# First group of two chunks, first batch's k and q ahead of v, another engine sequence in the MLP, two chunks a step in short tiles

## The chip, the core and the metric

The kernel runs on one core of a Trainium2 chip. The metric is the time of one execution on the device, in microseconds (us); the median over runs is compared. The engines are TensorE (PE in the profile, with its weight loads as PEld), VectorE (DVE), ScalarE (ACT), GpSimd (POOL) and SyncE (SP, which here issues nearly all DMAs). Each engine takes its own instructions in the order in which they are written.

## What is computed

Inputs are q, k, v of shape (4, 8, 576, 64), and weights. Heads 0 to 3 attend to the 32 latest positions, heads 4 to 7 to every fourth of the 128 latest. Two MLPs follow, over 2304 tokens.

```python
attn = softmax(where(mask, q @ k.T / 8, -1e9)) @ v     # batch 4, heads 8, 576 x 64
x = attn.transpose(0, 2, 1, 3).reshape(2304, 512)
h = x @ w_in                                           # 512 -> 2048
x = (h - tanh(h)) @ w_out                              # 2048 -> 512
out = (((x @ w1) * (x @ w2)) @ w3) @ wo                # 512 -> 1024 -> 1024 -> 512
```

## The kernel before

All matrix products of the MLPs are made of three: each operand stands as an upper part (`hi`, rounded to fp32r) and a lower part (`lo`, the rest), and hi·hi, hi·lo and lo·hi are added in PSUM (`mm3`).

**Weights** arrive as 64-bit floats, 512 KB a tile, and are converted on the core. One conversion is: a DMA into one of two `stage` buffers (`load64`), an absolute value on ScalarE (`cv_abs`, L105), four bit operations of 512 columns on VectorE (`cv_bits`, L110, L114, L120, L123), the upper part on ScalarE (L128) and the lower part on GpSimd (L129). `tick` moves this chain on by one stage: it splits the tile whose bits are done, does the bits of the next one, issues a load, and takes the absolute value of a loaded tile. There are 72 tiles. Their parts need two slots each; 16 slots (`WG`) exist from the start, 18 more (`LT`) come when attention's buffers are closed, and slots come free again when a tile has been used for the last time.

**Attention** is cut into 24 units, six for each batch (two kinds of heads, three blocks of positions). One unit has a k tile and a q tile (`load_q`, two DMAs, 224 KB at most and 384 KB), a v tile (`load_v`, two or four DMAs, 384 KB), scores on TensorE (`at_scores`: 1 mask product and 24 pairs of small matmuls), maximum and subtraction on VectorE (`at_max`), exp on ScalarE, the sum and its reciprocal on VectorE and the scaling on GpSimd (`at_norm`), three transposes on TensorE (`at_T`), their copy on ScalarE, the product with v on TensorE (`at_pv`), and its two parts written to X by ScalarE and VectorE (`at_evac`). An `attn_slot` does one stage each for four units that follow each other. k, q and v have three buffers each, so a load for unit n+3 waits until unit n has used its own.

**The first MLP** goes over 16 chunks of 128 hidden columns in four groups, `GS = (3, 4, 4, 5)`. For each group it goes over tiles of tokens, and in each tile over the group's chunks. The first group has six tiles of 256 tokens and two of 384, and its steps alternate with attention slots (`due` counts them); the other groups have four tiles of 512 and one short tile of 256. One step i is: 12 matmuls into `h` (`st_h`, L415), tanh on ScalarE (L449), h minus tanh on VectorE (`st_g`, L455), its upper part on ScalarE (L457), its lower part on VectorE (`st_glo`, L464; on GpSimd while attention runs), and, behind the next step's `st_h`, 12 matmuls into `y` (`st_y`, L492). After a tile's last chunk `y` is copied to Y (first group, L503 and L505) or added to it on VectorE (L507).

`start_up` handles the first batch's attention, and then this loop takes over:

```python
st_h(i)
st_tanh(i)
st_g(i)
st_glo(i)
...
if i:
    st_y(i - 1)
...
if g or i < 3 or i >= 18 or i % TE == 0:
    tick()
```

**The second MLP** first multiplies w3 and wo (8 steps of 24 matmuls), and then goes over five tiles of tokens with 8 steps each: two products into `h` (L415), their product on VectorE (L678), its parts (L680, L681) and 12 matmuls into the output (L697). The conversions that are left run beside its first tile.

## Time and profile before

| | us |
|---|---|
| median of 3 runs | 859.16 (858.43 to 860.78) |
| the profiled execution | 861.07 |
| its span | 859.3 |
| TensorE busy in the span | 819.1 |
| VectorE busy | 483.9 |
| ScalarE busy | 293.8 |
| GpSimd busy | 133.0 |

The span runs from the first to the last instruction; 1.77 us of the profiled execution lie around it. Busy time of TensorE includes stretches in which a matmul took longer than it must, so what TensorE loses is read from the times at which products start.

### The profile page before, as it was taken

The page shows a single profiled execution, that of the slowest core. Times are in us where ns is not written, and L with a number is a line of the kernel's source. Part 1 is how long each engine was busy: PE and PEld are TensorE (multiplying, and loading weights), DVE is VectorE, ACT ScalarE, POOL GpSimd, SP SyncE. Part 2 cuts the span into 40 slices and gives each one's busy share as a digit, 9 for nine tenths or more (in the row PEclk, how much of TensorE's full clock was granted, in tenths as well). Part 3 has the DMA queues.
Part 4 walks back from the last instruction along what each step waited for, and adds up shares of the span by engine and source line. Part 5 has one row for each costly group of instructions (what it writes and reads, how often), then busy time and mean ns, then how long its engine had stood idle before and what let it go on. Part 6 is the DMA issues. An engine that isn't in the chain of part 4 may idle for free.

```text
span 859.3 us, 13590 instructions
## 1 busy us (share of the span) xinstructions
PE 819.1 (95%) x5568; PEld 688.7 (80%) x5574; DVE 483.9 (56%) x789; ACT 293.8 (34%) x557; POOL 133.0 (15%) x120
## 2 busy tenths in 40 slices
PE   7588999999999999999999979999999999999998
PEld 4477999877789788888888878886788888888897
DVE  5588654888735873378888885577612212222121
ACT  3545655444422432234343333333311211211121
POOL 2243232222100210012211131222100000000000
PEclk9789999999999999999999999999999999999999
DMA  9978851222300320012322322133010010010010
GB/s 258 270 216 237 231 169 39 74 99 98 99 1 6 107 84 1 1 50 99 98 74 74 99 98 73 50 99 109 14 50 1 0 50 1 1 49 1 1 50 25
DMA packets 36511, 67.74 MB, mean 79 GB/s; under 512 B 4320, under 2 KB 24928, under 8 KB 36448
## 3 DMA queue, kind: packets, MB, share of 16 engines
q1 hardware_dynamic: 35456, 66.60, 25.5%
q8 instruction: 44, 0.72, 0.3%
q10 hardware_dynamic: 992, 0.26, 0.1%
q14 instruction: 19, 0.16, 0.1%
HBM read 62.13 MB, written 4.72 MB: 78 GB/s over the span
## 4 chain that ended last, share of the span: by engine, by line
PE 65%; DVE 21%; DMA 6%; ACT 5%; issue 2%; SPq 0%; ACTq 0%; DVEq 0%
PE h L415 37%; PE y L492 14%; PE o L697 10%; DVE a L110 4%; DVE a L114 3%; DVE a L120 3%; DVE a L123 3%; DVE th L455 2%; DVE gs L464 2%; ACT gs L457 2%; DMA st<-in_w 2%; PE x L353 2%; DMA v<-in_vt 2%; PE s L293 1%; DVE Y L507 1%
## 5 line engine op out<-in xcount | busy, mean ns | idle before, releaser
L415 PE MATMUL h<-X,LT 128*128 128x512 f32 (+1 forms) x576 | 131.3, 368 | 0.0
L492 PE MATMUL y<-gs,WG 128*128 128x256 f32 (+2 forms) x648 | 123.3, 338 | 5.0 <-DVE Y L507 3.0
L415 PE MATMUL h<-WG,X 128*128 128x512 f32 (+1 forms) x441 | 120.3, 375 | 0.0
L492 PEld LDWEIGHTS y<-gs,WG 128*128 128x128 f32 x648 | 102.4, 189 | 20.2 <-ACT WG L128 2.2
L415 PEld LDWEIGHTS h<-X,LT 128*128 128x128 f32 x576 | 101.5, 188 | 18.0
L415 PE MATMUL h<-X,WG 128*128 128x256 f32 (+2 forms) x567 | 113.9, 341 | 2.1 <-ACT X L369 1.2
L678 DVE TENSOR_TENSOR a_sb<-h,a_sb 128x512 f32<-128x512 f32 (+1 forms) x40 | 25.5, 638 | 158.5 <-PE h L415 152.3
L415 PEld LDWEIGHTS h<-X,WG 128*128 128x128 f32 x567 | 91.8, 196 | 11.7 <-ACT X L369 1.5
L492 PE MATMUL y<-gs,LT 128*128 128x512 f32 (+1 forms) x420 | 93.9, 373 | 5.7 <-ACT gs L457 4.6
L415 PEld LDWEIGHTS h<-WG,X 128*128 128x128 f32 x441 | 83.2, 189 | 15.2
L492 PEld LDWEIGHTS y<-gs,LT 128*128 128x128 f32 x420 | 74.4, 192 | 20.4 <-ACT gs L457 5.6
L455 DVE TENSOR_TENSOR th<-h,th 128x512 f32<-128x512 f32 (+2 forms) x89 | 52.1, 585 | 66.4 <-ACT th L449 66.3
L105 ACT ACTIVATE a<-st 128x512 f32<-128x512 f32 x72 | 48.5, 673 | 100.4 <-DMA st<-in_w 48.6
L457 ACT ACTIVATE gs<-th 128x512 fp32r<-128x512 f32 (+2 forms) x89 | 49.0, 550 | 92.9 <-DVE th L455 92.9
L449 ACT ACTIVATE th<-h 128x512 f32<-128x512 f32 (+2 forms) x89 | 45.4, 510 | 76.3 <-PE h L415 75.9
L464 DVE TENSOR_TENSOR gs<-th,gs 128x512 fp32r<-128x512 f32 (+2 forms) x71 | 44.9, 632 | 46.2 <-ACT gs L457 45.2
L415 PE MATMUL h<-LT,X 128*128 128x512 f32 (+1 forms) x198 | 60.6, 375 | 0.0
L114 DVE TENSOR_SCALAR a<-a 128x512 uint32<-128x512 uint32 x72 | 58.0, 805 | 2.5
L110 DVE TENSOR_SCALAR a<-a 128x512 f32<-128x512 f32 x72 | 59.0, 819 | 0.5 <-ACT a L105 0.5
L129 POOL TENSOR_TENSOR X<-a,X 128x512 fp32r<-128x512 f32 x26 | 35.6, 1367 | 130.5 <-ACT X L128 119.0
L123 DVE SCALAR_TENSOR_TENSOR a<-st,a 128x512 uint32<-128x512 uint32 x72 | 54.2, 753 | 2.5
L120 DVE SCALAR_TENSOR_TENSOR a<-st,a 128x512 uint32<-128x512 uint32 x72 | 53.6, 744 | 2.4
(69 smaller groups left out, 990.3 us busy)
## 6 DMA issues: line engine op xcount, KB each, us to landing
st<-in_w SPq DMA_DIRECT2D x32, 512.0 KB, 3.4
q<-in_qz SPq DMA_DIRECT2D x24, 384.0 KB, 5.1
st<-in_w_in SPq DMA_DIRECT2D x16, 512.0 KB, 3.5
st<-in_w_out SPq DMA_DIRECT2D x16, 512.0 KB, 3.5
v<-in_vt SPq DMA_DIRECT2D x32, 192.0 KB, 5.3
st<-in_wo SPq DMA_DIRECT2D x8, 512.0 KB, 3.4
k<-in_kT SPq DMA_DIRECT2D x16, 224.0 KB, 5.2
v<-in_vt SPq DMA_DIRECT2D x16, 128.0 KB, 3.6
```

What stands on the lines that cost most here:

```text
L105: nc.scalar.activation(out=a.bitcast(F32), in_=st[:, :, 1].bitcast(F32), func=ACTF.Abs)
L110: nc.vector.tensor_scalar(out=a.bitcast(F32), in0=a.bitcast(F32), scalar1=2.0 ** -15, scalar2=CMAX, op0=ALU.max, op1=ALU.min,)
L114: nc.vector.tensor_scalar(out=a, in0=a, scalar1=3, scalar2=0x3FFFFFFF, op0=ALU.logical_shift_left, op1=ALU.bitwise_and,)
L120: nc.vector.scalar_tensor_tensor(out=a, in0=st[:, :, 1], scalar=0xC0000000, in1=a, op0=ALU.bitwise_and, op1=ALU.bitwise_or)
L123: nc.vector.scalar_tensor_tensor(out=a, in0=st[:, :, 0], scalar=29, in1=a, op0=ALU.logical_shift_right, op1=ALU.bitwise_or)
L415: nc.tensor.matmul(out=ps, lhsT=a[sel[0]], rhs=b[sel[1]], start=(i == 0), stop=(i == n - 1), **kw)
L449: nc.scalar.activation(out=th[:, :tn], in_=gst[i][:, :tn], func=ACTF.Tanh)
L455: nc.vector.tensor_tensor(out=th[:, :tn], in0=ps[:, :tn], in1=th[:, :tn], op=ALU.subtract)
L457: nc.scalar.activation(out=gs[:, 0, :tn], in_=th[:, :tn], func=ACTF.Copy)
L464: eng.tensor_tensor(out=gs[:, 1, :tn], in0=th[:, :tn], in1=gs[:, 0, :tn].bitcast(F32), op=ALU.subtract)
L492: nc.tensor.matmul(out=y[k], lhsT=wt[sel[0]][:, 128 * k:128 * k + 128], rhs=gs[:, sel[1], :tn], start=(c == 0 and n == 0 and (not packed o ...
L697: nc.tensor.matmul(out=ps, lhsT=cs[:, e, 128 * m:128 * m + 128], rhs=WW[j][f], start=(j == 0 and n == 0), stop=(j == NJ - 1 and n == 2),)
```

## The change

- The first group has two chunks, the third five: `GS = (2, 4, 5, 5)`. The number of steps in the first group falls from 24 to 16, and 1.5 times as many attention slots stand in each.
- At the start, k and q of the first five units are issued ahead of any v; no buffer has to come free for them, since `homes` puts the first batch's v tiles, and k and q of its units 3 to 5, into parts of Y that nothing else uses yet. The first batch's attention is written out as a string of words (s scores, M maximum, E exp, N norm, T transposes, C copy, P product, O evacuation, a and b the two halves of the bit operations, f the split, z a spinning matmul). Unit 5 of the first batch moves into the slots behind.
- Mask tables and a copy of the identity are cast on GpSimd (before on VectorE and ScalarE), and ScalarE issues 10 DMAs for them (before 6).
- `tick` takes the slots before the bit operations, and unless `later` is set it splits the tile in the same call. In the second to fourth group it is called between `st_g` and `st_glo`. In a slot the transposes come ahead of the product with v.
- In short tiles of the second to fourth group a step takes two chunks: two times 12 matmuls into two halves of one `h` tile, then one tanh, one subtraction and one lower part of 512 columns, then two times 12 matmuls into `y`.
- In the second MLP's first tile the two calls of `tick` stand behind each other.

```diff
-GS = (3, 4, 4, 5)
+GS = (2, 4, 5, 5)
...
-    def tick():
+    def split():
+        key, a, hi, lo = bitsed.popleft()
+        cv_hi(a, hi)
+        cv_lo(a, hi, lo)
+        W[key] = (hi, lo)
+    def tick(later=False):
         if bitsed:
-            key, a = bitsed[0]
-            if len(free) - (reserve[0] if key[0] in ("w1", "w2") else 0) >= 2:
-                bitsed.popleft()
-                hi, lo = free.popleft(), free.popleft()
-                cv_split(a, hi, lo)
-                W[key] = (hi, lo)
-        if absed and not bitsed:
+            split()
+        if absed and len(free) - (reserve[0] if absed[0][0][0] in ("w1", "w2") else 0) >= 2:
             key, st, a = absed.popleft()
             cv_bits(st, a)
-            bitsed.append((key, a))
+            bitsed.append((key, a, free.popleft(), free.popleft()))
         prefetch()
         if loaded and not absed:
             key, st = loaded.popleft()
             absed.append((key, st, cv_abs(st)))
+        if bitsed and not later:
+            split()
...
-        attn_pools["pp"] = st.enter_context(tc.tile_pool(name="pp", bufs=3))
+        attn_pools["pp"] = st.enter_context(tc.tile_pool(name="pp", bufs=4))
...
-        for j in range(4):
-            r = slice(HQ * j, HQ * j + HQ)
-            nc.scalar.dma_start(out=m[r, 1:], in_=masks[r, 1:, 32 * (j % 2):32 * (j % 2) + HW])
+        nc.scalar.dma_start(out=id_sb, in_=ident)
         nc.scalar.dma_start(out=m[:, 0], in_=masks[:, 0, :HW])
-        nc.scalar.dma_start(out=id_sb, in_=ident)
+        for a in (slice(1, 2), slice(2, 6)):
+            for j in range(4):
+                r = slice(HQ * j, HQ * j + HQ)
+                nc.scalar.dma_start(out=m[r, a], in_=masks[r, a, 32 * (j % 2):32 * (j % 2) + HW])
...
+            nc.gpsimd.tensor_copy(out=mask_sb[:, to], in_=src)
+
+        if part == 0:
+            nc.gpsimd.tensor_copy(out=id16_sb, in_=id_sb)
+            put(slice(9, 10), m[:, 0:1])
+            put(slice(10, 13), m[:, 1:2])
+            return
...
+        if of_v:
+            if n < PB:
+                k, a = (0, wq * n) if n < 3 else (n - 2, c0)
+                return Y[:, k, a:a + wq].rearrange("p (h t c) -> p h t c", h=2, t=TU)
+            return attn_pools["kv"].tile([128, 2, TU, 2 * D], F32, tag="v", name="v")
+        if 3 <= n < PB:
+            a = Y[:, n - 2, c0 - wk - wq:c0]
+            k = a[:, :wk].rearrange("p (e k) -> p e k", e=2)
+            q = a[:, wk:].rearrange("p (e t c) -> p e t c", e=2, t=TU)
+        else:
...
+        if on[2]:
+            at_T(n - LAGT)
...
         if on[2]:
-            at_T(n - LAGT)
+            at_Tcopy(n - LAGT)
         if on[3]:
             at_evac(n - LAGP)
         if on[0]:
             at_max(n)
-        if on[2]:
-            at_Tcopy(n - LAGT)
-        if on[0]:
             at_exp(n)
...
+            w = 2 if g and tn == 256 else 1
+            for c in range(0, GS[g], w):
+                cs = list(range(c, min(c + w, GS[g])))
+                steps.append((g, ti, t0, tn, cs, ti == len(tiles) - 1))
...
+        for m, c in enumerate(cs):
+            key = ("in", sum(GS[:g]) + c)
+            wi = [w.rearrange("p (k f) -> p k f", k=KC) for w in W[key]]
+            mm3(ps[:, tn * m:tn * m + tn], [
+                ([w[:, k, :] for w in wi], [X[:, 2 * k + e, t0:t0 + tn] for e in range(2)])
+                for k in range(KC)
+            ], start=m == 0, skip_group_check=len(cs) > 1)
...
+        order = [(m, n, k) for m in range(len(cs)) for n in range(3) for k in range(KC)]
+        if cs[0] == 0 or cs[-1] == GS[g] - 1:
+            order.sort(key=lambda mnk: mnk[2])
...
-        ld(0)
-        load_q(0)
-        load_q(1)
-        load_q(2)
-        load_v(0)
-        ld(1)
-        prep_masks()
-        for part in range(2):
-            bits(0, part)
-        fin(0)
...
-        for n in range(PB + LAGP - 1):
-            if n < PB:
-                at_scores(n)
-                load_q(n + 3)
...
-            if n == 1:
-                load_v(2)
-                ld(2)
...
+        run("q0 w0 q1 q2 q3 q4 v0 v1")
+        run("m0 a0 b0 f0 m1")
+        run("w2 v2 v3 v4 w1 q5 v5")
+        run("""
+            s0 z1 s1 M0 E0 z1 M1 E1 s2 z1 N0 s3 M2 E2 z1 N1 T0 C0 z1 s4 M3 E3 T1 C1 P0 O0
+            N2 M4 E4 T2 C2 P1 N3 T3 C3 P2 a2 N4 O1 T4 C4 P3 b2 O2 P4 f2 a1 O3 O4 b1
+        """)
+        run("q6 q7 v6 v7")
...
-        slot[0] = PB
-        first[:] = [PB, PB, PB, PB - 1]
+            if m == 1:
+                hi, lo = free.popleft(), free.popleft()
+                bitsed.append((key, ab[m], hi, lo))
+        slot[0] = PB - 1
+        first[:] = [PB - 1] * 4
...
+                if g:
+                    tick()
+                elif i == 0:
+                    tick(True)
+                elif i == 1 and bitsed:
+                    split()
                 st_glo(i)
-                if i < 2:
-                    tick()
-                due += 0.75 if i < 6 else 0.5
+                due += 1.125 if i < 4 else 0.75
...
-            due += 0.75 if i < 6 else 0.5
+            due += 1.125 if i < 4 else 0.75
...
-            if g or i < 3 or i >= 18 or i % TE == 0:
-                tick()
+            if g == 0 and (i >= 12 or i % 2 == 0):
+                tick(True)
...
             nc.scalar.activation(out=hi, in_=ps, func=ACTF.Copy)
+            tick()
             nc.vector.tensor_tensor(out=lo, in0=ps, in1=hi.bitcast(F32), op=ALU.subtract)
...
-            tick()
...
                     tick()
+                    tick()
...
-            tick()
```

SyncE, in the start, from the second weight tile on: what it issues in the kernel before (`st` is a weight tile, `k`, `q`, `v` are attention's).

```order
L100 DMA st<-in_w_out 128x1024
L249 DMA k<-in_kT 128x2x192
L253 DMA q<-in_qz 128x2x384
L272 DMA v<-in_vt 64x2x384 x2
L249 DMA k<-in_kT 128x2x224
L253 DMA q<-in_qz 128x2x384
L272 DMA v<-in_vt 64x2x384 x2
L100 DMA st<-in_w_in 128x1024
L249 DMA k<-in_kT 128x2x224
L253 DMA q<-in_qz 128x2x384
```

And in the changed kernel, from the third unit's k and q on (`Y` stands for the parts of Y that hold k, q and v for a time).

```order
L274 DMA k<-in_kT 128x2x224
L277 DMA q<-in_qz 128x2x384
L274 DMA Y<-in_kT 128x2x192
L277 DMA Y<-in_qz 128x2x384
L274 DMA Y<-in_kT 128x2x224
L277 DMA Y<-in_qz 128x2x384
L296 DMA Y<-in_vt 64x2x128
L296 DMA Y<-in_vt 64x2x256
L296 DMA Y<-in_vt 64x2x128
L296 DMA Y<-in_vt 64x2x256
L296 DMA Y<-in_vt 64x2x384 x2
L100 DMA st<-in_w_in 128x1024
```

Before, v of unit 1 stands behind k and q of unit 3, and a second weight tile ahead of both; now five units' k and q, then two units' v, then the second weight tile.

VectorE, from one step to the next of the second group in the kernel before: the four bit operations stand behind the lower part `gs` of a step.

```order
L464 TENSOR_TENSOR gs<-th,gs 128x512
L110 TENSOR_SCALAR a<-a 128x512
L114 TENSOR_SCALAR a<-a 128x512
L120 SCALAR_TENSOR_TENSOR a<-st,a 128x512
L123 SCALAR_TENSOR_TENSOR a<-st,a 128x512
L455 TENSOR_TENSOR th<-h,th 128x512
```

And one step in the changed kernel:

```order
L490 TENSOR_TENSOR th<-h,th 128x512
L110 TENSOR_SCALAR a<-a 128x512
L114 TENSOR_SCALAR a<-a 128x512
L120 SCALAR_TENSOR_TENSOR a<-st,a 128x512
L123 SCALAR_TENSOR_TENSOR a<-st,a 128x512
L499 TENSOR_TENSOR gs<-th,gs 128x512
```

The four bit operations moved between the subtraction `th` and the lower part `gs` of the same step.

VectorE, in the short tile of the fourth group in the kernel before: a conversion stands between any two pairs of 256 columns.

```order
L455 TENSOR_TENSOR th<-h,th 128x256
L464 TENSOR_TENSOR gs<-th,gs 128x256
L110 TENSOR_SCALAR a<-a 128x512
L114 TENSOR_SCALAR a<-a 128x512
L120 SCALAR_TENSOR_TENSOR a<-st,a 128x512
L123 SCALAR_TENSOR_TENSOR a<-st,a 128x512
L455 TENSOR_TENSOR th<-h,th 128x256
L464 TENSOR_TENSOR gs<-th,gs 128x256
```

And in the changed kernel, the short tile's second and third step:

```order
L490 TENSOR_TENSOR th<-h,th 128x512
L110 TENSOR_SCALAR a<-a 128x512
L114 TENSOR_SCALAR a<-a 128x512
L120 SCALAR_TENSOR_TENSOR a<-st,a 128x512
L123 SCALAR_TENSOR_TENSOR a<-st,a 128x512
L499 TENSOR_TENSOR gs<-th,gs 128x512
L490 TENSOR_TENSOR th<-h,th 128x256
L110 TENSOR_SCALAR a<-a 128x512
L114 TENSOR_SCALAR a<-a 128x512
L120 SCALAR_TENSOR_TENSOR a<-st,a 128x512
L123 SCALAR_TENSOR_TENSOR a<-st,a 128x512
L499 TENSOR_TENSOR gs<-th,gs 128x256
```

A conversion now stands in a step of two chunks, whose two operations are 512 columns wide, and one in the last step of one chunk; the short tile has three steps in place of five, and two conversions in place of four.

## Rows read from the trace of the kernel before

**Rows 1.** Stretches: length, busy us of PE, PEld, DVE, ACT, POOL; clock, DMA, GB/s
```profile
0.00:42.00 42.00, 26.00 (x460) 17.10 (x467) 22.53 (x51) 17.43 (x36) 10.74 (x15) 0.86 0.95 265
42.00:86.00 44.00, 37.52 (x709) 32.96 (x708) 37.58 (x76) 23.16 (x52) 17.36 (x18) 0.90 0.80 227
86.00:147.00 61.00, 61.00 (x1104) 56.00 (x1102) 34.10 (x85) 34.95 (x79) 17.56 (x23) 1.00 0.55 154
147.00:172.00 25.00, 23.41 (x138) 22.09 (x132) 19.39 (x30) 11.04 (x23) 5.82 (x5) 1.00 0.20 64
172.00:230.00 58.00, 56.23 (x247) 45.59 (x248) 49.87 (x71) 25.11 (x46) 14.52 (x11) 1.00 0.30 100
```

**Rows 2.** Timeline of the start: start, length, engine, line, operation, idle before and its releaser
```profile
28.45 0.88 PE L293 MATMUL s<-k,q 128*32 128x64 f32 x48 [2.73 <-DMA q<-in_qz]
31.37 1.50 SPq L272 DMA_DIRECT2D v<-in_vt  x2
37.55 1.55 PE L353 MATMUL x<-pb,v 128*64 128x64 f32 x24 [2.24 <-DVE X L370]
41.56 2.50 PE L415 MATMUL h<-X,WG 128*128 128x256 f32 x10 [1.21 <-ACT X L369]
```

**Rows 3.** Timeline of TensorE: the first 384-column product
```profile
147.06 2.35 PE L415 MATMUL h<-X,WG 128*128 128x384 f32 x12
```

**Rows 4.** Chain of work that ended last: start, length, engine, tile, line
```profile
92.86 1.44 PE h L415 x12
98.14 1.44 PE h L415 x12
231.41 2.72 PE h L415 x12
```

**Rows 5.** Timeline of the short tile that ends the fourth group
```profile
486.39 1.59 PE L415 MATMUL h<-X,WG 128*128 128x256 f32 x12
503.55 1.70 PE L492 MATMUL y<-gs,LT 128*128 128x256 f32 x12 [1.53 <-ACT gs L457]
508.01 2.96 PE L492 MATMUL y<-gs,LT 128*128 128x256 f32 x12 [2.76 <-ACT gs L457]
510.77 1.03 PE L415 MATMUL h<-LT,X 128*128 128x512 f32 x2
```

**Rows 6.** Timeline of VectorE and GpSimd in the second group
```profile
199.53 1.29 POOL L129 TENSOR_TENSOR WG<-a,WG 128x512 fp32r<-128x512 f32 x1 [4.07 <-PE h L415]
199.57 1.53 DVE L110 TENSOR_SCALAR a<-a 128x512 f32<-128x512 f32 x1
207.32 0.42 DVE L110 TENSOR_SCALAR a<-a 128x512 f32<-128x512 f32 x1
```

**Rows 7.** Groups of instructions by form: count, busy us, mean ns, idle before
```profile
L110 DVE TENSOR_SCALAR a<-a 128x512 f32<-128x512 f32 x72 | 59.0, 819 | 0.5 <-ACT a L105 0.5
L120 DVE SCALAR_TENSOR_TENSOR a<-st,a 128x512 uint32<-128x512 uint32 x72 | 53.6, 744 | 2.4
L464 DVE TENSOR_TENSOR gs<-th,gs 128x512 fp32r<-128x512 f32 x52 | 36.0, 692 | 36.3 <-ACT gs L457 36.3
L305 DVE TENSOR_TENSOR pm<-s,ms 128x384 f32<-128x384 f32 x24 | 13.4, 558 | 2.2
L317 DVE RECIPROCAL ms<-ms 128x6 f32<-128x6 f32 x24 | 4.6, 191 | 0.8
L464 POOL TENSOR_TENSOR gs<-th,gs 128x256 fp32r<-128x256 f32 x18 | 13.2, 735 | 49.6 <-ACT gs L457 37.8 <-issue 11.8
L105 ACT ACTIVATE a<-st 128x512 f32<-128x512 f32 x72 | 48.5, 673 | 100.4 <-DMA st<-in_w 48.6 <-DMA st<-in_w_in 21.3 <-DMA st<-in_w_out 17.9
```

**Rows 8.** Timeline of TensorE at the start of the third group
```profile
284.87 3.00 PE L492 MATMUL y<-gs,LT 128*128 128x512 f32 x12 [1.08 <-DVE Y L507]
```

**Rows 9.** Waits of the whole run: us in total, times, longest
```profile
PE y L492 <- DVE Y L507: 4.1, 5, 1.3
```

**Rows 10.** Chain of work that ended last, in the second MLP's first tile
```profile
575.84 3.34 DMA st<-in_w
```

More of the change, by code (lines that the diff above doesn't have):

```diff
@@ L415, in mm3 @@
                 nc.tensor.matmul(
[L416 removed]
+                    out=ps, lhsT=a[sel[0]], rhs=b[sel[1]], start=(start and i == 0), stop=(i == n - 1), **kw
                 )
@@ L476, in st_y @@
     def st_y(i):
-        g, ti, t0, tn, c, last = steps[i]
-        need(("out", sum(GS[:g]) + c))
-        wt = W["out", sum(GS[:g]) + c]
+        g, ti, t0, tn, cs, last = steps[i]
+        need(*[("out", sum(GS[:g]) + c) for c in cs])
         packed = g == 0 and ti < 6
-        if c == 0:
+        if cs[0] == 0:
             gst["y"] = y_ps(tn)
```

129 lines of the change are left out of this document (54 added, 75 removed).

## The prediction

> **What bounds the kernel now.** I read the busy time by stretches first, then the timeline of each stretch in which TensorE is short of work, then the chain that ended last. From 230 us on TensorE stands nearly gapless: 12 matmuls of 512 columns take 2.72 us there, and in the first group's steady part a step with one attention slot takes 98.14 - 92.86 = 5.28 us, of which its two products take 1.44 each, so a slot costs TensorE 2.40 [rows 4]. A step of 512 columns is then 5.44 us and one of 256 is 2.88; for 384 I take the middle, 4.16. Whatever is over these figures is loss, and four places hold nearly all of it.
>
> The start, up to the first 384-column product at 147.06 [rows 3]. Until then there are 24 slots and 35 products of 256 columns (18 `h`, 17 `y`): 24 x 2.40 + 35 x 1.44 = 108.0. So 39.1 are lost. To 42 us the DMA engines are busy 95% of the time at 265 GB/s, the granted clock averages 0.86 (so it lay at the lower of its two levels, 1.2 of 2.4 GHz, for a part), and TensorE works 26 of 42 us; from 42 to 86 VectorE is busy 37.6 of 44 us, and after 86 no loss is left [rows 1]. In the start the scores wait 2.73 for a q, unit 4's v is issued only at 31.37, behind q tiles of the second batch, its product starts at 37.55 and the first `h` runs from 41.56 [rows 2].
>
> From 147 to 230 VectorE is the engine that is late: 69.3 of 83 us busy. The 138 matmuls of the first 25 us (12 of 256 columns, 126 of 384) need 23.3, the 247 of the next 58 (18 of 384, 229 of 512) need 55.0 [rows 1, 4], so 4.7 are lost.
>
> The short tile that ends the fourth group. From 486.39 to 510.77 stand five `h` and five `y` of 256 columns and one `y` of 512: 10 x 1.44 + 2.72 = 17.1 of 24.4 us; 7.3 are lost, with TensorE waiting up to 2.76 for the lower part's step [rows 5]. VectorE has a whole conversion there in each 2.88 us.
>
> At tile ends `y` waits for the additions to Y, 4.1 us in five places [rows 9]; one is 1.08 at the third group's start [rows 8].
>
> **The change, part by part.** The sum is made against the profiled execution, 861.07, which lies 1.9 above the median of the runs; I take 1.9 off at the end.
>
> *TensorE's own work.* The first group loses six steps of 256 and two of 384, the others gain four tiles of 512 and one of 256: -6 x 2.88 - 2 x 4.16 + 4 x 5.44 + 2.88 = -1.0. Two chunks in a step change no matmul.
>
> *Start-up.* Five units (about 1.02 MB each from the shapes) and three weight tiles of 0.52 MB must land before the first `h`: 6.65 MB, 25.1 us at 265 GB/s [rows 1], from 1.2 us on, and I add 1.7 for the last landing: 28. Behind that last tile (word w1 of the string) ScalarE takes its absolute value (0.67) ahead of units 3 and 4's evacuation, and VectorE two bit operations and two lower parts (0.42 each, 0.55 each) [rows 6, 7]. So the first `h` at about 30.5, where it now starts at 41.56. If that tile or ScalarE's ten DMA issues come later it is 34; if data flow at the rate of full DMA share, 28. The mask casts on GpSimd have no row. Each has 64 to 192 columns, so one costs between nothing and the 0.74 of a 256-column pass of two inputs [rows 7]; three of them stand ahead of the first scores, 0 to 2.2. I take 0: VectorE converts the first weight tile ahead of the first maximum anyway, and that is the cover; without it the 2.2 would fall on the path. The Trainium skill ("GPSIMD Engine Reference", Performance versus the Vector engine) speaks against this move: it has GpSimd about half as fast as VectorE on an elementwise pass. No run here shows that ratio for a cast; by it the three would cost an estimated 1.5, and the sum would be 1.5 higher were they on the path.
>
> *First group.* What remains from the first `h` to the first 384-column product is 24 x 2.40 + 23 x 1.44 = 90.7, less five slots already done: 78.7 for TensorE alone. VectorE has in that stretch 19 units with four passes of about 0.55 (the row with 0.558 stands for four alike) and two small ones of 0.19: 2.58 each, 49.0; 12 subtractions and 10 copies of 256 columns at about 0.4 (estimated from 0.69 for 512), 8.8; and five conversions of 3.12 each (two bit operations near 0.82, two near 0.75), 15.6: 73.4 in all [rows 7]. Between 42 and 86, the stretch now that is packed most like it, VectorE reached 85% [rows 1], so I take 73.4 / 0.854 = 86. The first 384-column product then starts at 30.5 + 86 = 116.5. TensorE alone would allow 109; at 75% for VectorE it is 128. The DMAs of 24 units and 8 weight tiles, 28.6 MB, need 108 us at 265 GB/s, so they follow close behind and do not set it.
>
> A conversion costs 3.12, and not the 2.2 of two passes at 0.42 and two at 0.69, because GpSimd's lower part runs into it: beside it L110 took 1.53, alone 0.42 [rows 6]. The Trainium skill ("SBUF — State Buffer", Who interferes with whom) makes this a lock: a VectorE pass in a mode that uses both of its ports, or with two SBUF inputs, and a GpSimd pass that reads SBUF keep each other out for a whole instruction. The two rows agree with that. In the first group `tick(True)` still splits ahead of the bits, so by rule and rows the price stays there; if the overlaps fell away the stretch would be 5 shorter.
>
> *147 to 230.* Two chunks of the second group instead of one are converted before it starts, and a conversion in a step no longer meets GpSimd's lower part, which now follows it. A step with a conversion then holds VectorE for 2.2 + 2 x 0.69, plus 0.7, its share of four additions in four steps: 4.3 against 5.44 [rows 6, 7]. I take 4 off of the 4.7 (between 2 and 4.7).
>
> *Short tiles.* One conversion now stands beside 5.76 us of TensorE's work, and VectorE needs 3.6 for it. I take 6.3 off of the 7.3; the last step has one chunk and still a conversion. Of the waits for Y, 2.4 (1.08 and 1.28 at two group starts).
>
> *Lower part behind the conversion.* From the end of `h` the third part of `y` needs tanh (0.67 at most, by the absolute value of as many columns), subtraction 0.69, bits 2.2, lower part 0.69 and some 0.3 of gaps, 4.6 [rows 6, 7]; TensorE has two other products, 5.44, in between. What is queued behind the bits on VectorE, the additions to Y, ends some 0.4 before the next tile's `y` asks. I charge 1.0 for all tile ends.
>
> *Second MLP.* A cycle of the first tile hangs on a load that waits for a stage buffer, 3.34 to land [rows 10]; two `tick`s in a row leave it, and one more conversion falls into it: I charge 1.5 (0 to 3).
>
> Sum: 116.5 + (861.07 - 147.06) + (4 x 5.44 + 2.88 - 2 x 4.16 = 16.3) - 4 - 6.3 - 2.4 + 1.0 + 1.5 = 836.6, against the median 1.9 less: 834.7, so 835.
>
> **The rivals.**
>
> *TensorE sets the first group.* The transposes ahead of the product with v and four `pm` buffers let VectorE run at over 93%; the product at 109, the whole 7.5 less: 827. For it speaks the gapless stretch from 86 on [rows 1]; against it that no conversions ran there. Chance 0.22.
>
> *The first group stays as slow as VectorE or the loads make it.* More slots in a step put more GpSimd passes against the conversions, and SyncE's queue holds q and v behind a weight load that waits for VectorE. Then the product comes at 125 to 129 and the time is 843 to 848. For it speaks 42 to 86 [rows 1]. Chance 0.22.
>
> *The tiles' ends keep their stalls*, as the last step of one chunk and the group starts are still late: start as forecast, 6 of 8.7 given back, 841. Chance 0.07; with it go small mishaps of the start.
>
> *Slower: the lower part comes too late for `y` in the second to fourth group.* The place is L499 behind the four bit operations. It decides from a chain of 5.9 us on (5.44 and the 0.45 until the third matmul at tile ends), that is if a conversion takes 3.6 in place of 2.2, as when GpSimd blocks two of its four passes. To undo all of the gain of 24 it would have to wait 0.6 in each of some 39 steps with a conversion, a chain of 6.5; with 0.7 the time is 862. Against it: the lower part of the tile before ends long before the next bits. Chance 0.04.
>
> **How the numbers follow.** The forecast has 0.45: 835, its own range 830 to 841. The range of 8 in 10 goes from 823 (first 384-column product at 107 to 109, all losses gone, no charge) to 850 (that product at 128, half the charges more). A measurement of this kernel tells some 0.3%, 2.6 us. All cases but the last are faster by far more; for the last and for what I have not seen I give slower 0.04 and the same 0.03.
>
> **What would show it.** Right: first `h` near 30 and the first 384-column product near 116; no TensorE wait over 1 us in the fourth group's short tile; L110 near 0.42 in the second to fourth group and up to 1.5 in the first. Wrong: the first product over 34, VectorE under 80% in a first group that is still late, or `y` waiting for L499 in steady steps.

## The result and the profile after

The changed kernel takes 866.65 us (median of 8 runs, 862.25 to 868.12), the kernel before, run beside it, 859.81. The ratio is 1.0073, 95% interval 1.0054 to 1.0092: slower by 0.7%, where the forecast was 835 and faster, with a range of 823 to 850. The profiled execution took 865.26, 28.7 over the sum of 836.6 that was made for it.

The first product and the first 384-column product in the changed kernel's timeline (start, duration, engine, line; in brackets the idle time before and what ended it):

```profile
35.73 1.24 PE L442 MATMUL h<-X,WG 128*128 128x256 f32 x3
...
140.04 2.35 PE L442 MATMUL h<-X,WG 128*128 128x384 f32 x12 [1.18 <-DVE X L399]
```

They answer to 41.56 and 147.06 before [rows 2, 3]; at 41.56 start ten of the first product's 12 matmuls, the other two ran at 39.58, so the start was 3.9 earlier by its first matmul. The changed kernel by stretches (busy time of each engine, granted clock, DMA share, GB/s), which answers to [rows 1]:

```profile
0.00:36.00 36.00, 24.36 (x406) 15.81 (x411) 17.17 (x39) 13.80 (x26) 10.36 (x21) 0.88 0.92 263
36.00:140.00 104.00, 86.88 (x1720) 74.33 (x1720) 71.38 (x161) 53.80 (x123) 32.33 (x37) 0.94 0.72 197
158.00:180.00 22.00, 18.02 (x67) 14.07 (x66) 15.44 (x26) 9.53 (x17) 5.40 (x4) 0.84 0.31 95
180.00:230.00 50.00, 50.00 (x222) 41.40 (x221) 30.61 (x52) 19.11 (x31) 9.03 (x7) 1.00 0.25 74
490.00:515.00 25.00, 23.93 (x162) 22.12 (x161) 19.73 (x37) 9.91 (x17) 6.46 (x5) 1.00 0.33 106
580.00:620.00 40.00, 36.03 (x147) 27.80 (x146) 27.20 (x39) 15.67 (x27) 10.26 (x8) 0.96 0.25 79
```

TensorE's longest waits over the whole span (waiting tile and line, what ended the wait: us in total, times, longest):

```profile
PE t L355 <- POOL pm L342: 14.6, 8, 2.4
PE t L355 <- DMA Y<-in_vt: 6.4, 2, 3.2
PE o L714 <- ACT cs L697: 4.0, 3, 2.3
PE y L527 <- ACT Y L539: 3.7, 1, 3.7
```

Of the 28.7, the start is 5.2 (35.73 for 30.5) and the first group 18.3 (104.3 for 86). Behind the first 384-column product 5.1 are left, nearly all between 158 and 180, where TensorE is idle 4.0 and the clock lay at the lower of its two levels for a part (mean 0.84). The short tile is what the forecast said: 1.1 idle from 490 to 515. Two of the prediction's own signs of being wrong came: the first product over 34, and VectorE under 80% in a late first group (71.38 of 104.00 us, 69%).

The slot that shows the first group's trouble, from the same timeline (L110 to L123 are the conversion, L490 and L492 the subtraction from `h` and its upper part, L339 the sums, L342 GpSimd's product, L355 the transposes, L362 their copies, L398 and L399 the evacuation, L327 the next maximum):

```profile
103.80 0.42 DVE L110 TENSOR_SCALAR a<-a 128x512 f32<-128x512 f32 x1
...
105.45 1.67 DVE L123 SCALAR_TENSOR_TENSOR a<-st,a 128x512 uint32<-128x512 uint32 x1
...
107.03 0.41 DVE L490 TENSOR_TENSOR th<-h,th 128x256 f32<-128x256 f32 x1
...
107.37 0.54 DVE L339 TENSOR_REDUCE ms<-pm 128x6 f32<-128x384 f32 x1
107.48 0.42 ACT L492 ACTIVATE gs<-th 128x256 fp32r<-128x256 f32 x1 [1.59 <-DVE th L490]
...
107.80 0.98 ACT L362 ACTIVATE pb<-t 64x384 f32<-64x384 f32 x2
...
108.66 0.82 POOL L342 TENSOR_TENSOR pm<-pm,ms 128x384 f32<-128x384 f32 x1
108.80 0.49 ACT L398 ACTIVATE X<-x 128x384 fp32r<-128x384 f32 x1
...
109.32 0.56 DVE L399 TENSOR_TENSOR X<-x,X 128x384 fp32r<-128x384 f32 x1 [0.99 <-ACT X L398]
...
109.54 0.86 PE L355 MATMUL t<-id_sb,pm 128*128 128x128 f32 x3 [2.42 <-POOL pm L342]
...
109.80 0.55 DVE L327 TENSOR_REDUCE ms<-s 128x6 f32<-128x384 f32 x1
```

A conversion holds VectorE from 103.80 to 107.1. Behind it stand the subtraction from h, for which ScalarE waits 1.59, and the sums, for which GpSimd's product and then TensorE's transposes wait (2.42). On ScalarE the two copies of the transposes (L362, 0.98) come ahead of the evacuation (L398), so VectorE, done with the sums at 108.3, waits 0.99 for the evacuation, and the next maximum starts only at 109.80. From 36 to 140 VectorE's waits for that evacuation add up to 16.2:

```profile
DVE X L399 <- ACT X L398: 16.2, 19, 2.2
```

In the kernel before the same wait is 11.2 in nine times, two of them (2.7 and 2.0) at the end of the start and six of 0.9 from 97 us on, where TensorE runs without a gap [rows 1], so that they cost nothing:

```profile
DVE X L370 <- ACT X L369: 11.2, 9, 2.7
```

In the changed kernel the wait stands in 19 slots, in the same queue as the conversions, and no busy share shows it. What it costs there is tested by e13 and e14.

### The profile page after: what moved, and what is told of

Its sections match the earlier page's. It is cut to its first block, busy times and chain, and to the rows that moved or that the text cites. A ratio compares the mean times of both kernels' runs of the same rounds, so it can differ in the third digit from the quotient of the medians.

```text
span 863.5 us, 13422 instructions
## 1 busy us (share of the span) xinstructions
PE 820.9 (95%) x5497; PEld 687.4 (80%) x5501; DVE 440.3 (51%) x774; ACT 291.6 (34%) x534; POOL 126.1 (15%) x122
## 4 chain that ended last, share of the span: by engine, by line
PE 77%; DVE 10%; DMA 5%; ACT 4%; issue 2%; POOL 1%; SPq 0%; ACTq 0%; POOLq 0%; DVEq 0%
PE h L442 44%; PE y L527 20%; PE o L714 10%; DMA st<-in_w 2%; DVE a L123 2%; DVE a L120 2%; PE x L382 1%; DVE a L114 1%; DMA st<-in_w_out 1%; PE s L317 1%; DVE a L110 1%; DMA k<-in_kT 1%; DVE th L490 1%; ACT pb L362 1%; PE t L355 1%
## 5 line engine op out<-in xcount | busy, mean ns | idle before, releaser
L442 PE MATMUL h<-WG,X 128*128 128x512 f32 (+1 forms) x525 | 136.4, 371 | 0.0
L490 DVE TENSOR_TENSOR th<-h,th 128x512 f32<-128x512 f32 (+2 forms) x80 | 50.9, 636 | 132.6 <-ACT th L484 132.6
L527 PE MATMUL y<-gs,WG 128*128 128x512 f32 (+2 forms) x552 | 111.4, 351 | 4.0 <-ACT Y L539 3.7
L442 PE MATMUL h<-X,WG 128*128 128x512 f32 (+2 forms) x564 | 113.8, 348 | 1.2 <-DVE X L399 1.2
L442 PEld LDWEIGHTS h<-WG,X 128*128 128x128 f32 x525 | 95.0, 188 | 17.1
L527 PE MATMUL y<-gs,LT 128*128 128x512 f32 (+1 forms) x480 | 105.3, 368 | 1.6 <-DVE gs L499 1.1
L527 PEld LDWEIGHTS y<-gs,WG 128*128 128x128 f32 x552 | 91.7, 194 | 17.6 <-ACT Y L539 4.1
L442 PEld LDWEIGHTS h<-X,WG 128*128 128x128 f32 x564 | 92.7, 191 | 14.4 <-DVE X L399 1.3
L484 ACT ACTIVATE th<-h 128x512 f32<-128x512 f32 (+2 forms) x80 | 44.1, 552 | 132.2 <-PE h L442 131.8
L492 ACT ACTIVATE gs<-th 128x512 fp32r<-128x512 f32 (+2 forms) x80 | 47.3, 591 | 66.5 <-DVE th L490 66.5
L131 POOL TENSOR_TENSOR LT<-a,LT 128x512 fp32r<-128x512 f32 x25 | 32.6, 1303 | 184.2 <-ACT LT L128 153.7
L442 PE MATMUL h<-WG,LT 128*128 128x512 f32 (+1 forms) x225 | 57.6, 368 | 0.0
L499 DVE TENSOR_TENSOR gs<-th,gs 128x512 fp32r<-128x512 f32 (+2 forms) x68 | 45.7, 672 | 18.4 <-ACT gs L492 18.4
L123 DVE SCALAR_TENSOR_TENSOR a<-st,a 128x512 uint32<-128x512 uint32 x72 | 53.7, 745 | 2.5
L694 ACT ACTIVATE a_sb<-h 128x512 f32<-128x512 f32 (+1 forms) x40 | 22.0, 551 | 94.5 <-PE h L442 94.5
L714 PE MATMUL o<-X,cs 128*128 128x512 f32 x216 | 52.6, 391 | 0.7 <-ACT cs L697 0.7
```

The costliest lines, as they stand in the source:

```text
L123: nc.vector.scalar_tensor_tensor(out=a, in0=st[:, :, 0], scalar=29, in1=a, op0=ALU.logical_shift_right, op1=ALU.bitwise_or)
L131: nc.gpsimd.tensor_tensor(out=lo, in0=a.bitcast(F32), in1=hi.bitcast(F32), op=ALU.subtract)
L442: nc.tensor.matmul(out=ps, lhsT=a[sel[0]], rhs=b[sel[1]], start=(start and i == 0), stop=(i == n - 1), **kw)
L484: nc.scalar.activation(out=th[:, :tn], in_=gst[i][:, :tn], func=ACTF.Tanh)
L490: nc.vector.tensor_tensor(out=th[:, :tn], in0=ps[:, :tn], in1=th[:, :tn], op=ALU.subtract)
L492: nc.scalar.activation(out=gs[:, 0, :tn], in_=th[:, :tn], func=ACTF.Copy)
```

## The experiments

All ratios are against the kernel before on the same chip (its medians 859.6 to 860.4). "384" is where the first 384-column product starts in the profile; with three chunks in the first group (*) more of the work lies ahead of it. The column comes from one execution each: kernels with the same start have their first `h` anywhere from 34.9 (e4) to 38.8 (e12), so differences of up to some 4 in it tell nothing by themselves.

| run | edit | us | ratio (95%) | 384 |
|---|---|---|---|---|
| changed | | 866.65 | 1.0054 to 1.0092 | 140.0 |
| e1 | transposes last | 868.96 | 1.0074 to 1.0116 | 144.3 |
| e2 | no conversion behind the first group's last step | 860.45 | 0.9988 to 1.0025 | 140.9 |
| e3 | transposes one slot later | 864.00 | 1.0023 to 1.0054 | 141.6 |
| e4 | three chunks first | 862.13 | 1.0005 to 1.0044 | 153.6* |
| e5 | conversions in halves | 860.44 | 0.9999 to 1.0028 | 135.1 |
| e6 | split right behind the bits | 866.88 | 1.0052 to 1.0102 | 140.5 |
| e7 | three passes of four left out | 861.21 | 1.0005 to 1.0034 | 135.0 |
| e8 | loads unit by unit | 874.23 | 1.0144 to 1.0194 | 149.6 |
| e9 | conversions in odd steps | 865.71 | 1.0052 to 1.0084 | 141.8 |
| e10 | e9 and e2 | 859.03 | 0.9987 to 1.0005 | 141.9 |
| e11 | before, with the later groups' part | 846.82 | 0.9844 to 0.9873 | 144.4* |
| e12 | ticks apart | 865.85 | 1.0044 to 1.0081 | 143.9 |
| e13 | evacuation first | 859.84 | 0.9986 to 1.0016 | 133.9 |
| e14 | slot of before | 854.98 | 0.9911 to 0.9961 | 133.7 |
| e15 | e13, e5 and e2 | 850.05 | 0.9853 to 0.9902 | 130.5 |
| e16 | e11 and two chunks | 848.29 | 0.9845 to 0.9894 | 130.0 |
| e17 | e14, e5 and e2 | 846.58 | 0.9823 to 0.9866 | 127.3 |
| e18 | e14 and e2 | 848.21 | 0.9851 to 0.9901 | 126.7 |

### Which part is it: e1 to e4

**e1**, transposes behind the scores, the rest of the slot as changed:

```diff
-        if on[2]:
-            at_T(n - LAGT)
         if on[3]:
             at_pv(n - LAGP)
...
         if on[2]:
+            at_T(n - LAGT)
             at_Tcopy(n - LAGT)
```

> The changed kernel with one thing put back: in an attention slot the transposes stand behind the product with v and the scores again, not ahead of them. Theory A (order): in the first group TensorE waits at the head of a slot for GpSimd's product pm, 14.6 us in 8 waits on the matmul line of the transposes, because a conversion on VectorE holds up the sums that this product needs; behind two other pieces of work of about 2 us together the transposes find it done. Then these waits fall below 4 us, the first 384-column product comes at 127 to 131 in place of 140.0, and the time is 854 to 858. Theory B (VectorE's conversions with one and a half slots to a step are too much whatever the order): the waits move to the product with v or to the scores, the first 384-column product stays within 2 of 140 and the time within 3 of 866.7. The transposes' copies on ScalarE come closer to the next slot's product with v; if that is what counts, new waits of x for pb appear.

Theory A failed: the time is no better, and the waits moved to the product with v, which now waits for the copies (`x` for `pb`, 12.1 us in 8 waits).

**e2**, one conversion fewer ahead of the second group:

```diff
-            if g == 0 and (i >= 12 or i % 2 == 0):
+            if g == 0 and i < 15 and (i >= 12 or i % 2 == 0):
                 tick(True)
```

> The changed kernel without the conversion that follows the last step of the first group, so that two conversions no longer stand next to each other ahead of the second group's first y. Theory A (two conversions in a row, with their absolute values waiting for DMA ahead of the copies to Y on ScalarE): the wait of 3.67 us of y for ScalarE's copies to Y near 168 goes, the granted clock stays at 1.00 where it fell to 0.84 between 158 and 180, and the time falls by 5 to 8, to 859 to 862. Rival (the loads are late there, so the wait returns one step on): no more than 2 less, 865. All conversions come one step later after it; a tail of waits at the second MLP's start could give 1 back.

As theory A said, 6.2 less. In the changed kernel's timeline two conversions stand in a row there. ScalarE waits for the loads of two tiles ahead of its copies to Y, and `y` waits for those copies:

```profile
161.99 0.68 ACT L105 ACTIVATE a<-st 128x512 f32<-128x512 f32 x1 [2.11 <-DMA st<-in_w_in]
...
166.82 0.67 ACT L105 ACTIVATE a<-st 128x512 f32<-128x512 f32 x1 [1.76 <-DMA st<-in_w_out]
...
167.91 0.84 ACT L539 ACTIVATE Y<-y 128x384 f32<-128x384 f32 x2
...
168.44 5.49 PE L527 MATMUL y<-gs,WG 128*128 128x512 f32 x12 [3.67 <-ACT Y L539]
```

Behind the idle 3.67 the 12 matmuls took 5.49 in place of 2.72 [rows 4]. In e2 that `y` starts at 165.79, right behind its `h`, and the same stretch by engines is

```profile
158.00:180.00 22.00, 21.51 (x96) 17.21 (x94) 16.57 (x29) 10.95 (x20) 5.28 (x4) 1.00 0.31 95
```

**e3**, one more slot of distance:

```diff
-    LAGN, LAGT, LAGP = 1, 2, 3
+    LAGN, LAGT, LAGP = 1, 3, 4
```

> The changed kernel with one more slot between the sums and the transposes (transposes three slots behind the scores in place of two, the product with v four in place of three; five pm buffers, three ms). The order in a slot and VectorE's work stay. Theory A (the transposes stand too near behind the sums for a conversion to fit between): the 14.6 us that transposes wait for GpSimd's product go to below 2, the first 384-column product comes at 127 to 132 (one more slot lies ahead of the last product with v), the time is 854 to 859. Theory B (VectorE itself is too slow there): the waits move to the scores' buffers, the product stays near 140 and the time within 3 of 866.7.

Theory A failed: only 2.7 less, and the transposes still wait, now for the copies of the slot before out of the one PSUM tile (at 110.82 they start 0.09 behind those copies' end). The copies stand in ScalarE's queue behind the copy of `h` that the conversion holds up.

**e4**, chunks and rates of before:

```diff
-GS = (2, 4, 5, 5)
+GS = (3, 4, 4, 5)
...
-                due += 1.125 if i < 4 else 0.75
+                due += 0.75 if i < 6 else 0.5
...
-            if g == 0 and (i >= 12 or i % 2 == 0):
+            if g == 0 and (i < 3 or i >= 18 or i % 2 == 0):
```

> The changed kernel with the chunks of before (3, 4, 4, 5 in the four groups) and with them the rate of one slot a step that before had; start-up, transposes first, lower part behind the conversion, two chunks a step in short tiles all stay. In the steady first group no conversion is left then, since the weights' places are full, and slots stand 5.28 apart. If the loss lies in the first group of two chunks (conversions beside one and a half slots a step): from 35.7 there are 19 slots and 35 products, 96.0, so the first 384-column product comes at 131 to 136, and the time is 839 to 845. If the transposes at the head of a slot cost by themselves, waits for GpSimd's product remain in most slots, the product comes at 140 to 145 and the time is 848 to 853. If the new start-up is itself the loss, the first h comes later than 37 and the time is over 850.

None of the three. Behind 92 us all slots took 5.3 as before, but from 40 to 63 us, where three chunks want their conversions, two slots came 10.3 and 12.5 behind the one before them; there ScalarE waits 2.68 and 3.67 for loads of weight tiles.

### What a conversion costs: e5 to e7, e9, e10

Between the scores of one slot and those of the next the changed kernel takes 3.88 with one product in between and 5.32 with two: 2.44 without the products. With a conversion in the interval these 2.44 become 4.2 to 6.4; in five intervals behind the first `h` that is 14.4 more together.

**e5**, the bit operations in halves, first half behind even steps and second half behind odd ones:

```diff
+            if g == 0 and 2 <= i < 12:
+                half_tick(i % 2)
+            elif g == 0 and i != 1:
+                tick(True)
```

> The changed kernel with VectorE's conversions of the first group, from its third step on, cut in two: two of the four passes behind one step, the other two behind the next. The work is the same; the longest piece that stands ahead of the sums and the subtraction of a step falls from about 3.3 us to 1.6 to 2.3. Theory C (a conversion in one piece holds up two chains in order at once: the subtraction, which ScalarE's copies of h and of the transposes wait for, and the sums, which GpSimd's product and the transposes wait for): TensorE's waits at transposes fall from 14.6 to about 7, the first 384-column product comes at 132 to 136 in place of 140.0, and the time is 859 to 862. Rival D (the sum of the work of VectorE or of the transfers sets the pace): the product stays within 2 of 140 and the time within 3 of 866.7.

**e7**, of the four passes only the last:

```diff
+                part[0] = 2 if 2 <= i < 12 else None
                 tick(True)
```

> The changed kernel with three of VectorE's four passes left out in the conversions of the first group from its third step on (those weights are wrong), so four conversions hold VectorE for 0.7 to 1.7 in place of 3.3 each. Theory C: the waits of transposes after 80 us go, and the first 384-column product comes at 129 to 133, 7 to 11 earlier; the time is 856 to 860. Rival (the loads, GpSimd or one and a half slots a step hold TensorE by themselves): no more than 3 earlier, time over 863.

Both bring the first 384-column product 5 forward, although e7 takes 2.5 us of VectorE's work out of each conversion and e5 none: the sum of VectorE's work does not set the pace. That the length of the piece ahead of the chains sets it fits both, but was not varied further. And in both, from 60 us on, a third of the intervals stays 1.1 to 2.4 too long, so something else holds the slot.

**e6**, split behind the bits:

```diff
-                tick(True)
+                tick(i >= 12)
```

> The changed kernel with the split of a tile right behind its bit operations in the first group too, as in the later groups, so that GpSimd's lower part of one tile no longer runs beside the bit operations of the next, which took VectorE 1.66 for a pass of 0.69. Theory C: a conversion holds VectorE 2.3 in place of 3.3, four times, and the first 384-column product comes 3 to 5 earlier, time 862 to 864. Against it: ScalarE's upper part now waits for the bit operations ahead of the next tanh, and GpSimd's lower part of 1.3 comes closer ahead of the product of the sums, so that what VectorE gains GpSimd loses; then the time is 866 to 869.

Nothing gained. From 80 to 126 L123 did fall from 1.66 to 0.69, as GpSimd no longer ran beside it:

```profile
L123 DVE SCALAR_TENSOR_TENSOR a<-st,a 128x512 uint32<-128x512 uint32 x3 | 2.1, 692 | 0.1
```

The Trainium skill ("SBUF — State Buffer", Who interferes with whom) has VectorE and GpSimd lock each other out of a shared port; the two values agree with that. The edit moved no time, against the prediction's "5 shorter", but it does not price the lock by itself: ScalarE's upper part and the tanh behind it now wait for the bit operations, so the subtraction starts 3.30 behind the first of them (104.54 to 107.84) where it was 3.23 (103.80 to 107.03). That the lock is not the loss is shown below by e18, which has it still.

**e9**, conversions behind odd steps, where two products follow, and **e10**, the same with e2:

```diff
-            if g == 0 and (i >= 12 or i % 2 == 0):
+            if g == 0 and (i >= 12 or i == 0 or i % 2 == 1 and i > 1):
```

> The changed kernel with the first group's conversions behind the odd steps in place of the even ones from the third step on, where TensorE has two products between two slots and not one. Theory C (a conversion lies in the chains of the slot behind it; an interval between slots with a conversion holds 1.7 to 4.0 us more of TensorE's time than one without): with two products, 2.88 us, between the slots instead of 1.44, VectorE has about 1.4 more to finish in, so each of four conversions costs 1 to 1.5 less; the first 384-column product comes at 133 to 136, the time is 859 to 862. Rival (VectorE's sum of work): no change, 864 to 868.

> The same with the conversion behind the first group's last step taken out as well. Theory: the two places are apart and their gains add up (6.2 for the latter, 5 to 7 for the former), 853 to 856, below the kernel before at 859.8. If they don't add (the loads come late behind the moved conversions), 858 to 861.

Theory C failed here. The intervals with the conversion became free (5.32), and the two behind took 3.0 more together in two of three places (5.78 and 4.98 for 3.88). The delay was only passed on: VectorE's queue had no slack in any interval. e2's gain came on top (6.7).

### Start and later groups: e8, e11, e12

**e8**, each v behind the next unit's k and q:

```diff
-        run("q0 w0 q1 q2 q3 q4 v0 v1")
+        run("q0 w0 q1 v0 q2 v1")
...
-        run("w2 v2 v3 v4 w1 q5 v5")
+        run("q3 v2 w2 q4 v3 v4 w1 q5 v5")
```

> The changed kernel with the first loads unit by unit again: each v of the first five units stands behind the k and q of the unit after it, not behind all five; what is computed keeps its order. If the start is set by bytes (265 GB/s, all of five units and three weights ahead of the first h), the first h stays at 34.7 to 36.7 and the time within 3 of 866.7. If the late v are the loss (TensorE waits 3.2 twice for a v), the first h comes at 31 to 33 and the time falls by 3 to 4, to 863.

Both were wrong: the first `h` came at 44.1 and the time rose by 7.6; the scores wait 6.8 for a q in three places. The same bytes in another order are 8 slower, so the bytes alone do not set the start, and k and q ahead of v are a gain with this order of words.

**e11**, the kernel before with the change in the second to fourth group (and the new `tick`):

```diff
+            w = 2 if g and tn == 256 else 1
...
                 st_g(i)
+                if g:
+                    tick()
                 st_glo(i)
```

> The kernel before with the later part of the change alone: two chunks a step in short tiles, the lower part of gs behind the conversion in the second to fourth group, the split right behind the bits there, two conversions in a row in the second MLP's first tile; chunks (3, 4, 4, 5), start-up, slots and first group are those of before. The conversion behind the first group's last step is left out, since with the new order two would stand in a row there. Theory: the later part gives what the first group takes: the short tile 6, the groups' starts 3.5, the second group's first tile 2 to 3, less 2 in the second MLP, so 848 to 852, ratio 0.986 to 0.991. If the later part is itself a loss or nothing, 857 to 862.

13.0 faster than before. The second MLP stands in this edit as before; the two conversions in a row there, which the expectation counts, are not in it. TensorE idles 2.1 in all from 140 to 230, and 0.9 from 490 to 515:

```profile
490.00:515.00 25.00, 24.14 (x125) 20.64 (x125) 13.55 (x26) 8.24 (x15) 5.16 (x4) 1.00 0.25 85
140.00:230.00 90.00, 87.91 (x464) 76.59 (x459) 65.56 (x110) 41.48 (x75) 20.90 (x17) 1.00 0.28 88
```

**e12**, the second MLP's ticks as before:

```diff
                 if t == 0:
                     tick()
-                    tick()
...
+            tick()
```

> The changed kernel with the second MLP's two conversion steps of a cycle apart again, one ahead of the output product and one behind it. Theory: two in a row leave a load that waits for a stage buffer on the path; TensorE loses 7.1 between 580 and 620, before 4.9; apart again the time falls by 2, to 864.5. If the loss there comes from the split right behind the bits, no change, 866 to 868.

0.8 less, inside the intervals: no effect of their order is shown.

### The order on ScalarE: e13 to e18

**e13**, one pair of steps in the slot:

```diff
-        if on[2]:
-            at_Tcopy(n - LAGT)
         if on[3]:
             at_evac(n - LAGP)
         if on[0]:
             at_max(n)
+        if on[2]:
+            at_Tcopy(n - LAGT)
```

> The changed kernel with one pair of ScalarE's steps in a slot put back: the evacuation of x stands ahead of the copies of the transposes, as it did before; the transposes stay at the slot's head. Theory E (order on ScalarE): the change puts two copies of 0.49 each ahead of the evacuation, VectorE's subtraction from x waits 0.4 to 1.0 for it in each slot, and the next maximum stands behind that wait; so VectorE is occupied for some 3.6 of the 3.9 us of an interval, though it is busy 68%, and a conversion finds no gap. Without the wait a slot takes 0.5 to 0.9 less of VectorE: the conversions' price falls from 14.4 to some 9, the first 384-column product comes at 134 to 137, the time is 860 to 863. Rival (the pace is set by the chain scores, maximum, exponential, sums, product, transposes, whatever ScalarE's order): 140 and 865 to 868; the copies, later now, could make the product with v wait for pb.

**e14**, this and the transposes behind the scores, so the slot of before:

```diff
-        if on[2]:
-            at_T(n - LAGT)
         if on[3]:
             at_pv(n - LAGP)
...
+        if on[2]:
+            at_T(n - LAGT)
         if on[3]:
             at_evac(n - LAGP)
```

> The changed kernel with the whole slot of before: product with v, scores, transposes on TensorE, evacuation, copies, exponential on ScalarE. The run with the transposes last kept the copies ahead of the evacuation, so it was not yet this order. Theory E: as with the evacuation first, 860 to 863, and TensorE's waits for pb (12.1 us with the transposes last) fall below 5. Rival (two chunks and one and a half slots a step are slow in any order of the slot): 865 to 869.

Theory E held: 6.8 less in e13, a little better than its range. e14 is 11.7 less, 5 below its range: the transposes' place has a share that the theory had not counted. The wait for the evacuation from 36 to 140 (16.2 as changed), in e13 and then in e14:

```profile
DVE X L399 <- ACT X L398: 6.1, 4, 2.8
```

```profile
DVE X L399 <- ACT X L398: 3.3, 3, 1.8
```

The two orders belong together: with the copies ahead, the transposes' old place gave nothing (e1, 868.96); with the evacuation ahead, it gave another 4.9.

**e15**, e13 with e5 and e2; **e16**, e11 with the chunks and rates of the change; **e17** and **e18**, e14 with e2, e17 also with e5. In e15 and e17, in e18, and in e16 the lines beside those above are

```diff
-            elif g == 0 and i != 1:
+            elif g == 0 and i not in (1, 15):
...
-            if g == 0 and (i >= 12 or i % 2 == 0):
+            if g == 0 and i < 15 and (i >= 12 or i % 2 == 0):
...
-GS = (3, 4, 4, 5)
+GS = (2, 4, 5, 5)
```

> The changed kernel with three edits: the conversions of the first group in halves (alone 6.2 less), none behind the first group's last step (alone 6.2 less), evacuation ahead of the copies. If the three add up: 850 to 854; if the third gives nothing, 854 to 856. In both cases below the kernel before, and above the 846.8 of the later part alone on the old first group.

> The kernel before with the later part of the change (846.8) and now the chunks (2, 4, 5, 5) and the changed kernel's rates of slots, but the start-up, the slot and the order of loads of before. It tells the chunks from the start-up. If a first group of two chunks is itself the loss, as slots stand closer and each conversion lands on TensorE's path: 851 to 858. If the loss comes from the new start-up and slot: 843 to 848, the first 384-column product at 126 to 131 (16.3 of TensorE's work stand behind it instead of ahead).

> The changed kernel with the slot of before, the first group's conversions in halves, and none behind the first group's last step. By the runs so far the slot is worth 11.7 and the last step 6.2; the halves were worth 6.2 where each conversion cost 2.9, and with the slot of before a conversion costs about 1.1, so 1 to 3 of it are left: 844 to 849. If the halves give nothing here, 848 to 850. Against the later part alone on the old first group (846.8) it is then about the same, so the changed start and chunks would be worth nothing even when repaired.

> The same without the halves: the changed kernel with the slot of before and no conversion behind the first group's last step. If the two places add up, 866.65 - 11.7 - 6.2 = 848.8, so 847 to 851; if not, 851 to 855.

The gains add up in e17 and e18, which came in the ranges for that case. e15 (850.05) did too, though the three gains alone make 847.4. e16 (848.29) came just over its second case, with its first 384-column product at 130.0 inside: a first group of two chunks by itself costs 1.5 over e11, inside the intervals, and is not the loss. In e18 the stretch of the first group has almost the work that it has as changed, in 92 us for 104:

```profile
35.00:127.00 92.00, 81.10 (x1724) 71.13 (x1723) 70.46 (x162) 55.42 (x123) 31.89 (x37) 0.99 0.82 225
```

VectorE is busy 77% there, for 69% as changed, and an interval with a conversion takes 0.98 over the others (4.81 for 3.83). Yet from 80 to 126 GpSimd still runs beside L123, which takes 1.71, so the lock was not what made a conversion dear:

```profile
L123 DVE SCALAR_TENSOR_TENSOR a<-st,a 128x512 uint32<-128x512 uint32 x3 | 5.1, 1708 | 0.1
```

The profile is of e18's fastest execution (845.34, median 848.21). e14, whose program is the same up to there, was profiled in its slowest (857.56, median 854.98): the stretch took 96.9, with one stall of TensorE from 72 to 76 that no edit explains. e17's halves are within the interval of e18.

## Why the prediction was wrong

The runs close the account of the change. Second to fourth group -13.0 (e11), two chunks +1.5 (e16 less e11), new start, mask casts and the second MLP's ticks together -0.1 (e18 less e16; this and the 1.5 are inside the intervals), the new slot +11.7 (e14), two conversions in a row at the second group's start +6.2 (e2): +6.3, where 6.8 was measured.

- **First group: wrong, and the step that failed is "VectorE reached 85% (...) so I take 73.4 / 0.854 = 86".** The work was right (71.4 busy for 73.4). The rate was 69%: it was taken from the slot of before and given to a slot of another order. The change put the copies ahead of the evacuation on ScalarE, and VectorE waits for the evacuation in the middle of its slot; that wait is idle time, but nothing can use it. This order costs 6.8 (e13), and the transposes' earlier place, which the prediction held to be a help in a rival, another 4.9 (e14). But with the slot of before the stretch is 91.7 in e18 and 96.9 in e14, not 86: VectorE reached 77% and 73% there. So the order is 7 to 13 of the 18.3, and the other 6 to 11 are the rate itself, which one stretch of the kernel before does not give to another. What holds those is not shown by an experiment; in e18 most intervals stand at TensorE's own pace (3.83), those with a conversion 0.98 over it, and one, at 41 us, takes 8.23.
- **The rival of a slow first group** (843 to 848) had the sign and not the cause: it spoke of GpSimd against the conversions, and e18 is fast with that overlap in place; and of q and v held up behind weight loads, where TensorE has one wait of 1.2 for a load from 36 to 140.
- **147 to 230, "I take 4 off of the 4.7": wrong.** The step asked what VectorE has to do in a step, and did not follow ScalarE's row at the second group's start, where two conversions meet. Without the second, 6.2 come back.
- **Start: 35.73 for 30.5.** The bytes alone did not set it (e8: the same bytes, 44.1). VectorE's words stand behind waits: it waits 2.70 for an evacuation that ScalarE has behind copies (word O0, ahead of N2), and 3.73 for an absolute value (word a2, ahead of N4), and both times the transposes wait for the sums behind:

```profile
21.20 0.56 DVE L399 TENSOR_TENSOR X<-x,X 128x384 fp32r<-128x384 f32 x1 [2.70 <-ACT X L398]
...
28.29 0.43 DVE L110 TENSOR_SCALAR a<-a 128x512 f32<-128x512 f32 x1 [3.73 <-ACT a L105]
...
29.10 0.54 DVE L339 TENSOR_REDUCE ms<-pm 128x6 f32<-128x384 f32 x1
...
30.24 0.83 POOL L342 TENSOR_TENSOR pm<-pm,ms 128x384 f32<-128x384 f32 x1 [4.71 <-DVE ms L341]
...
31.12 0.90 PE L355 MATMUL t<-id_sb,pm 128*128 128x128 f32 x3 [3.21 <-DMA Y<-in_vt]
```

  The row names a DMA, but the transposes start 0.05 after GpSimd's product ends at 31.07. Another order of these words was not tried, so this is argued from rows only.
- **Mask casts at nothing: right.** The three ahead of the first scores took 0.29, 0.24 and 0.35, together 0.88, and the scores start at 9.35. The Trainium skill ("GPSIMD Engine Reference", Performance versus the Vector engine) has GpSimd at about half of VectorE's rate on an elementwise pass, an addition of two inputs, from which the prediction estimated 1.5 for these casts of one; the traces have less.
- **Short tile, waits for Y, lower part behind the conversion: right or better.** The charge of 1.0 at tile ends was not needed, nor did the slower rival's late lower part show. From 180 to 480 L110 and L123 took 0.42 and 0.69 on average, so no longer beside GpSimd. In the second MLP 4.0 are idle from 580 to 620 (before 2.9), where 1.5 was charged; putting the ticks apart gave 0.8.
- **TensorE's own work, -1.0,** was not measured by itself: two chunks came out at +1.5 with all they bring, inside the intervals.

e17 (846.58), e11 (846.82), e18 and e16 (848.2, 848.3), e15 (850.05) and e14 (854.98) beat both kernels. e11 does so without the new start, the new slot and the new chunks.

## What to carry to other kernels

Where engines take instructions in order, price an edit by what stands behind each wait, engine by engine, and not by busy shares: a rate read from one order of instructions does not hold for another, and here it did not hold for the same order in another stretch (85% read, 73 to 77% reached). Two engines that hand results to each other within a slot should take the hand-over in the same order; here one swapped pair cost 6.8 us, and with the transposes' place 11.7. If a delay moved to a place with slack comes back one interval later, the queue has no slack, and the wait inside it is what to look for.

## What the runs showed of the hardware

- GpSimd's casts from f32 to bf16 took 0.24 us for 64 columns, 0.29 for 128 and 0.35 for 192, on 128 partitions (changed kernel).
- An idle stretch of 3.67 on TensorE was followed by 12 matmuls at half speed (5.49 for 2.72, granted clock 0.50 from 168.4 to 174.0), so the lower clock cost 2.8 on top of the wait.
- A VectorE pass (L123) took 1.66 beside GpSimd's lower part and 0.69 without it (changed kernel and e6, 80 to 126 us). e18 gained 18.4 over the changed kernel with that pass still at 1.71.
